# Gate and up products of a SwiGLU block by Strassen's scheme, with float32r operand sums

## The chip, the cores and the metric

The kernel runs on one core of one Trainium2 chip. The metric is device time in microseconds (us) of one execution, as the median of several runs. The profile is of one execution. Its engines are PE (TensorE, matmuls; PEld is its weight load), DVE (VectorE), ACT (ScalarE), POOL (GpSimd) and SP (SyncE, which here only starts DMAs). Each engine works through its own list of instructions in order; between engines there are semaphores.

## The reference

x is 2048 x 512. It is normalised row by row, and two branches of the result are added to x:

```
xn = layernorm(x)
q, k, v = xn @ wqkv                       # 32 heads of 16
pq, pk  = phi(q), phi(k)                  # phi(t) = (t > 0 ? t + 1 : exp(t)) + 1e-6
o = pq (pk^T v) / (pq . sum(pk))          # per head: linear attention
out = x + o @ wo + (silu(xn @ w_gate) * (xn @ w_up)) @ w_down     # hidden width 1792
```

Inputs and output are bf16.

## The kernel before

The 2048 rows are 16 tiles of 128 (t), or 4 chunks of 512 (C = t // 4). The hidden width is 14 pieces of 128 (fc). Everything is written out by hand: a small recorder (`K.add`) takes operations in the order of the text, with the keys that each reads and writes, gives every engine its operations in that order, and derives the semaphore waits. So the order of the text is the order of each engine's list, and an operation that waits holds up all that stands behind it on its engine.

The first stage (0 to about 46 us) is a hand-made list of two-character steps: layernorm of each tile (`bn1`, `bn2`, `rs`, `lna_dve`, `lna_pool`), transposition of the normalised tile into xnT by DMA, projections to q and k (`proj`, line 423), phi (`phi_exp` on ACT, `phi_min` on POOL, `phi_sum` on DVE, line 462), and the accumulation of G = xn^T pk in PSUM banks 0 to 3 (`gacc`, line 472). The projections go round banks 4 to 7. At the end of the list the first gate/up pairs (`pair`) stand between the last G accumulations.

The second stage loops over 56 pairs j = (chunk C, piece fc). A pair is 4 matmuls for gate and 4 for up (`gu`, line 526; stationary a 128x128 piece of the weights, moving 512 columns of xnT), a silu on ACT (line 534) and a product on DVE (`hop`, line 539) that writes a 128x512 piece of hT. The pairs use banks 4 and 5, or 6 and 7, in turn. hT holds two chunks. Between the pairs stand the matmuls of kv (line 584), its mask, M = kv @ wo (line 650), the sum of pk over all rows (z: `z_add` on POOL and DVE, line 495), the denominators (`pz_mul` on POOL, line 617; `divide` and `scale_turn` on DVE, lines 624 to 639), and, from the second chunk on, the output tiles of the chunk before: `ogroup` takes 4 matmuls with M (line 656) and 14 with w_down (line 660) for a tile, `oout` adds x and stores (line 666). z is summed in two halves; of the three tiles whose pk is kept unscaled (0, 1 and 2), `z_add` scales 0 and 1.

Weights and x come by DMAs that SP starts, in the order of the list (`BIG`): w_gate and w_up in halves, the v part of wqkv, wo, and w_down.

Of the kernel before, what the change touches and what calls it, by code (L numbers as in the profile page):

```python
# [6 lines left out]
dt = mybir.dt  # L7
# [22 lines left out]
O_SLOT = {5: 0, 8: 1, 11: 2, 13: 3}  # L30
PZ_AT = {13 + 11 * t // 4: t for t in range(16)}
DIV_AT = {j + 1: t for j, t in PZ_AT.items()}


class _Program:
# [3 lines left out]
    def __init__(self):  # L39
        self.ops = []  # L40
        self.last_w = {}
        self.readers = {}

    def add(self, eng, fns, r=(), w=(), dma=False):
# [4 lines left out]
        for k in r:  # L49
            if k in self.last_w:  # L50
                deps.add(self.last_w[k])
        for k in w:
            if k in self.last_w:
                deps.add(self.last_w[k])
            deps |= self.readers.get(k, set())
        keep = []
        for d in deps:
            o = self.ops[d]
            if o["eng"] == eng and not o["dma"]:
                raw = any(self.last_w.get(k) == d for k in r)  # L60
                if eng == "pe" or not (raw or dma):
                    continue
            keep.append(d)
            o["inc"] = True
# [3 lines left out]
        for k in w:  # L68
            self.last_w[k] = i
            self.readers[k] = set()  # L70
        return i
# [40 lines left out]
def bass_parallel_sum__linear_attn_block__swiglu_ffn__prompt_kernel(nc, A_x, A_wqkv, A_wo, B_x, B_w_gate, B_w_up, B_w_down, out):  # L112
# [5 lines left out]
    with contextlib.ExitStack() as es:  # L118
# [5 lines left out]
        x_sb = sb("x_sb", [P, NT, D], bf)  # L124
        xn = sb("xn", [P, NT, D], bf)
# [7 lines left out]
        xnT = sb("xnT", [P, NDC, S], bf)  # L133
        wqkv = sb("wqkv", [P, NDC, 3 * D], bf)
        wo = sb("wo", [P, NG, D], bf)
        wg = sb("wg", [P, NDC, F], bf)
        wu = sb("wu", [P, NDC, F], bf)
        wd = sb("wd", [P, NFC, D], bf)
        pk = sb("pk", [P, NT, D], bf)
        pq = sb("pq", [P, NT, D], bf)  # L140
        hT = sb("hT", [P, 2, NFC, 512], bf)
        zacc = sb("zacc", [P, 2, D], f32)
        zb = sb("zb", [P, D], bf)
        ef = sb("ef", [P, 6, D], bf)
        GT = sb("GT", [P, NDC, D], bf)
# [3 lines left out]
        pz = sb("pz", [P, 2, D], f32)  # L149
        den = sb("den", [P, 2, NH], f32)  # L150
        rden = sb("rden", [P, 2, NH], f32)
        sil = sb("sil", [P, 2, 512], bf)
        out_sb = sb("out_sb", [P, 2, D], bf)
        ident = sb("ident", [P, P], bf)
        zT = sb("zT", [P, NG, P], bf)
# [9 lines left out]
        xc = hT[:, 1, 0:NC, :]  # L165
        xg = hT[:, 1, NC:2 * NC, :]
        xcT = hT[:, 1, 2 * NC:3 * NC, :].rearrange("p a b -> p (a b)").rearrange("p (c s) -> p c s", c=NDC)
        junk = [hT[:, 1, 3 * NC + t, :] for t in CENTRED]
        zt = pz[:, 0, :]
        shared = {(1, t): [("xc", t, 0), ("xc", t, 1)] for t in CENTRED}  # L170
        shared.update({(1, NC + t): [("xg", t)] for t in CENTRED})
        shared.update({(1, 2 * NC + a): [("xcT", t, h) for t in CENTRED for h in (0, 1)] for a in CENTRED})
        shared.update({(1, 3 * NC + t): [("junk", t)] for t in CENTRED})
        later = {}
        tq = [hT[:, 0, 2 * i:2 * i + 2, :].rearrange("p a b -> p (a b)").bitcast(f32) for i in range(NFC // 2)]
        shared.update({(0, q): [("tq", q // 2)] for q in range(NFC)})
# [22 lines left out]
        def fload(eng, key, dst, src, h):  # L199
            load(eng, (key, h), dst[:, :, h * FH:(h + 1) * FH],  # L200
                 src[:, h * FH:(h + 1) * FH].rearrange("(c p) f -> p c f", p=P))
# [151 lines left out]
        def evac(t, b, eng="act", lo=0, hi=NDC):  # L353
            src = tview(b, hi - lo)
            dst = (xcT if t in CENTRED else xnT)[:, lo:hi, t * P:(t + 1) * P]
# [40 lines left out]

        def xkeys(t):
            return [("xnT", t)]

        def dmat(t):  # L400
            K.add("sp", lambda e: e.dma_start_transpose(out=xnT[:, :, t * P:(t + 1) * P], in_=xn[:, t, :]),
# [11 lines left out]
        def proj(i, t, cs):  # L413
# [4 lines left out]
            src = xcT if t in CENTRED else xnT  # L418
            fns = []
            for c in cs:  # L420
# [3 lines left out]
                    banks[b][:, :], src[:, c, t * P:(t + 1) * P], wqkv[:, c, col:col + D], start=first, stop=last))  # L424
# [6 lines left out]
        def phi_keep(t):  # L431
            b, slot = at[0, t], later[t]
            K.add("act", lambda e: e.activation(tq[slot], banks[b][:, :], ACT.Copy), r=[B(b)], w=[("tq", slot)])

        def phi_exp(i, t):
            b = at[i, t]
            buf, bkey = ef[:, efslot(b), :], ("ef", efslot(b))
            if i == 0 and t in later:
                buf, bkey = pq[:, t, :], ("pq", t)
# [6 lines left out]
        def phi_min(i, t):  # L446
            buf, bkey = ef[:, efslot(at[i, t]), :], ("ef", efslot(at[i, t]))
            if i == 0 and t in later:
                buf, bkey = pq[:, t, :], ("pq", t)
# [5 lines left out]
        def phi_sum(i, t):  # L455
            b = at[i, t]
            dst, dkey = ((pk[:, t, :], ("pk", t)) if i else (pq[:, t, :], ("pq", t)))
            low, lkeys = (flo[:, t:t + 1], [("flo", t)]) if t in CENTRED else (1e-6, [])
            val, mid, keys = banks[b][:, :], ef[:, efslot(b), :], [B(b), ("ef", efslot(b))]
            if i == 0 and t in later:  # L460
                val, mid, keys = tq[later[t]], pq[:, t, :], [("tq", later[t]), ("pq", t)]
            K.add("dve", lambda e: e.scalar_tensor_tensor(  # L462
                out=dst, in0=val, scalar=low, in1=mid, op0=ALU.max, op1=ALU.add),
# [4 lines left out]
        def gacc(t):  # L468
# [4 lines left out]
                banks[c][:, :], src[:, t, c * P:(c + 1) * P], pk[:, t, :],  # L473
# [4 lines left out]
        NZP = 10  # L478

        def z_add(half, i):  # L480
            acc, key = zacc[:, half, :], ("zacc", half)
            t = NZP * half + i
            if half == 0 and i == 1:
                K.add("pool", lambda e: e.tensor_scalar(
                    out=acc, in0=pk[:, 0, :], scalar1=rstd[:, 0:1], scalar2=0.0, op0=ALU.mult, op1=ALU.add),
                    r=[("pk", 0), ("rs", 0)], w=[key])
                K.add("pool", lambda e: e.tensor_scalar(
                    out=zt, in0=pk[:, 1, :], scalar1=rstd[:, 1:2], scalar2=0.0, op0=ALU.mult, op1=ALU.add),
                    r=[("pk", 1), ("rs", 1)], w=[("pz", 0)])
                K.add("pool", lambda e: e.tensor_tensor(out=acc, in0=acc, in1=zt, op=ALU.add),  # L490
                      r=[key, ("pz", 0)], w=[key])
                return
            first, fkey = (pk[:, t - 1, :], ("pk", t - 1)) if i == 1 else (acc, key)
            K.add("dve" if half else "pool",
                  lambda e: e.tensor_tensor(out=acc, in0=first, in1=pk[:, t, :], op=ALU.add),  # L495
                  r=[fkey, ("pk", t)], w=[key])

        def stat(t):
# [14 lines left out]
            "Q": lambda t, cs=range(NDC): proj(0, t, cs), "y": lambda t: phi_exp(0, t), "z": phi_keep, "n": lambda t: phi_min(0, t), "u": lambda t: phi_sum(0, t), "G": gacc, "F": lambda t: keep_busy(t, 256),  # L513
        }

        def gb(j):
            return 4 + 2 * (j % 2)

        def gu(j, extra=(), er=(), ew=()):
            C, fc = j // NFC, j % NFC  # L520
            n = (len(extra) + 7) // 8
            todo = list(extra)
            for b, w_, key in ((gb(j), wg, "wg"), (gb(j) + 1, wu, "wu")):
                fns = []
                for c in range(NDC):
                    fns.append(lambda e, c=c, b=b, w_=w_: e.matmul(  # L526
                        banks[b][:, :], w_[:, c, fc * P:(fc + 1) * P], xnT[:, c, C * 512:(C + 1) * 512],
# [231 lines left out]
```

## Time and profile before

| | |
|---|---|
| three runs | 211.48, 211.82, 211.95 us (median 211.82) |
| span of the profiled execution, first to last instruction | 210.5 us |
| time of the profiled execution beside its span | not given apart from the span |
| PE busy | 207.9 us, 1012 matmuls |
| DVE busy | 124.4 us, 223 instructions |
| ACT busy | 67.2 us, 137 instructions |
| POOL busy | 66.0 us, 92 instructions |
| gate and up matmuls (line 526) | 448 |
| mean granted TensorE clock | 1.000 |

A row of a group reads: line, engine, operation, output <- inputs, shapes, count | busy time in us, mean ns of one | idle time of the engine just before them, and what ended it. A row of the chain or of the timeline begins with its start and its length in us; a timeline row may merge several like instructions (x4). Matmuls are pipelined, so the 379 ns of one overlap with the next.

### The profile page before, as it was taken

Reading aid. Unit: us, or ns where it says so; the run is one execution under the profiler, and the core shown is the slowest. Engines: PE = TensorE matmul, PEld = TensorE weight load, DVE = VectorE, ACT = ScalarE, POOL = GpSimd, SP = SyncE. Lnnn points to the kernel's source line nnn. Section 1 sums busy time; section 2 is a strip of 40 time slices with the busy share of each in tenths; the row PEclk is TensorE's granted clock in tenths of the full one; section 3 lists DMA queues with packets and bytes.
Section 4 is the critical chain, followed back from the end, with each engine's and each line's share of the span. In section 5 each row is a group of like instructions: output and inputs, shape, how many; then the busy total and the mean of one; then the engine's idle time right before and its main releaser. Section 6 shows DMA issues by size and latency. Waiting matters only on the chain.

```text
span 210.5 us, 2725 instructions
## 1 busy us (share of the span) xinstructions
PE 207.9 (99%) x1012; PEld 96.7 (46%) x1012; DVE 124.4 (59%) x223; ACT 67.2 (32%) x137; POOL 66.0 (31%) x92
## 2 busy tenths in 40 slices
PE   8999999999999999999999999999999999999996
PEld 4444444444544444444444444444444444444455
DVE  3999999625995377464554774464457473625122
ACT  5985566644255333021221322130123031220000
POOL 3498876569930152202202121202202220000000
PEclk9999999999999999999999999999999999999999
DMA  5974568699201302010101120111010112011101
GB/s 164 360 231 97 138 101 188 132 344 367 108 0 25 53 0 43 7 50 28 25 25 50 25 30 25 25 50 25 28 31 19 25 50 51 3 50 28 47 28 50
DMA packets 28733, 16.43 MB, mean 78 GB/s; under 512 B 18608, under 2 KB 28592, under 8 KB 28720
## 3 DMA queue, kind: packets, MB, share of 16 engines
q1 hardware_dynamic: 27856, 15.48, 27.8%
q10 hardware_dynamic: 864, 0.79, 1.3%
q8 instruction: 8, 0.13, 0.3%
q14 instruction: 5, 0.04, 0.1%
HBM read 9.96 MB, written 2.10 MB: 57 GB/s over the span
## 4 chain that ended last, share of the span: by engine, by line
PE 99%; DVE 0%; issue 0%
PE pb L526 46%; PE pb L660 23%; PE pb L423 13%; PE pb L656 7%; PE pb L472 7%; PE pb L241 2%; PE pb L384 0%; PE pb L584 0%; PE pb L650 0%; PE pb L376 0%; PE pb L350 0%; DVE out_sb L666 0%
## 5 line engine op out<-in xcount | busy, mean ns | idle before, releaser
L534 ACT ACTIVATE sil<-pb 128x512 bf16<-128x512 f32 x56 | 33.4, 597 | 104.9 <-PE pb L526 103.4
L539 DVE TENSOR_TENSOR hT<-pb,sil 128x512 bf16<-128x512 f32 x56 | 38.2, 683 | 38.0 <-PE pb L526 37.5
L526 PE MATMUL pb<-xnT,wg 128*128 128x512 bf16 x224 | 57.8, 379 | 0.0
L526 PE MATMUL pb<-xnT,wu 128*128 128x512 bf16 x224 | 57.8, 379 | 0.0
L660 PE MATMUL pb<-wd,hT 128*128 128x512 bf16 (+2 forms) x252 | 51.4, 355 | 0.0
L617 POOL TENSOR_TENSOR pz<-pq,zbc 128x512 f32<-128x512 bf16 x16 | 22.3, 1394 | 91.7 <-DVE den L624 79.0
L660 PEld LDWEIGHTS pb<-wd,hT 128*128 128x128 bf16 x252 | 23.5, 98 | 25.0
L526 PEld LDWEIGHTS pb<-xnT,wu 128*128 128x128 bf16 x224 | 21.9, 98 | 25.9
L526 PEld LDWEIGHTS pb<-xnT,wg 128*128 128x128 bf16 x224 | 21.9, 98 | 25.8 <-DVE pq L462 0.2
L666 DVE TENSOR_TENSOR out_sb<-pb,x_sb 128x512 bf16<-128x512 f32 (+2 forms) x18 | 11.4, 633 | 35.8 <-PE pb L660 35.8
L423 PE MATMUL pb<-wqkv,xnT 128*128 128x512 bf16 x104 | 23.9, 379 | 0.0
L444 ACT ACTIVATE ef<-pb 128x512 bf16<-128x512 f32 x26 | 15.1, 593 | 11.6 <-PE pb L423 11.6
L451 POOL TENSOR_SCALAR ef<-ef 128x512 bf16<-128x512 bf16 x26 | 15.9, 618 | 8.5 <-ACT ef L444 8.5
L656 PE MATMUL pb<-M,pk 128*128 128x512 bf16 (+2 forms) x72 | 16.8, 355 | 0.0
L423 PEld LDWEIGHTS pb<-wqkv,xnT 128*128 128x128 bf16 x104 | 10.1, 98 | 12.4 <-issue 0.3
L251 DVE BATCH_NORM_STATS2 stats<-x_sb 128x6 f32<-128x512 bf16 x16 | 10.9, 678 | 3.5 <-DMA x_sb<-in_A_x_dram 3.4
L472 PE MATMUL pb<-pk,xn 128*128 128x512 bf16 x52 | 12.7, 379 | 0.0
L639 DVE TENSOR_TENSOR pq<-pq,rden 128x512 bf16<-128x512 bf16 x16 | 12.6, 786 | 0.0
L624 DVE TENSOR_REDUCE den<-pz 128x32 f32<-128x512 f32 x16 | 10.8, 675 | 0.0
L462 DVE SCALAR_TENSOR_TENSOR pq<-pb,ef 128x512 bf16<-128x512 f32 x13 | 8.7, 679 | 3.0 <-POOL ef L451 3.0
L462 DVE SCALAR_TENSOR_TENSOR pk<-pb,ef 128x512 bf16<-128x512 f32 x13 | 8.9, 683 | 2.7 <-POOL ef L451 2.7
L495 POOL TENSOR_TENSOR zacc<-zacc,pk 128x512 f32<-128x512 f32 x8 | 10.2, 1279 | 0.6
(72 smaller groups left out, 109.5 us busy)
## 6 DMA issues: line engine op xcount, KB each, us to landing
out_dram<-out_sb SPq DMA_DIRECT2D x15, 128.0 KB, 1.7
x_sb<-in_A_x_dram SPq DMA_DIRECT2D x14, 128.0 KB, 4.5
wu<-in_B_w_up_dram SPq DMA_DIRECT2D x2, 896.0 KB, 9.0
wg<-in_B_w_gate_dram SPq DMA_DIRECT2D x2, 896.0 KB, 8.9
wd<-in_B_w_down_dram SPq DMA_DIRECT2D x1, 1792.0 KB, 10.7
wqkv<-in_A_wqkv_dram ACTq DMA_DIRECT2D x4, 128.0 KB, 4.9
wqkv<-in_A_wqkv_dram SPq DMA_DIRECT2D x4, 128.0 KB, 4.7
wqkv<-in_A_wqkv_dram SPq DMA_DIRECT2D x1, 512.0 KB, 4.9
```

Source lines behind the costliest of these rows:

```text
L423: fns.append(lambda e, c=c, first=first, last=last: e.matmul(banks[b][:, :], src[:, c, t * P:(t + 1) * P], wqkv[:, c, col:col + D], start= ...
L444: K.add("act", lambda e: e.activation(buf, banks[b][:, :], ACT.Exp), r=[B(b)], w=[bkey])
L451: K.add("pool", lambda e: e.tensor_scalar(out=buf, in0=buf, scalar1=top, scalar2=0.0, op0=ALU.min, op1=ALU.max), r=[bkey] + tkeys, w=[bkey])
L462: K.add("dve", lambda e: e.scalar_tensor_tensor(out=dst, in0=val, scalar=low, in1=mid, op0=ALU.max, op1=ALU.add), r=keys + lkeys, w=[dkey])
L472: K.add("pe", [(lambda e, c=c: e.matmul(banks[c][:, :], src[:, t, c * P:(c + 1) * P], pk[:, t, :], start=first, stop=last)) for c in range ...
L526: fns.append(lambda e, c=c, b=b, w_=w_: e.matmul(banks[b][:, :], w_[:, c, fc * P:(fc + 1) * P], xnT[:, c, C * 512:(C + 1) * 512], start=(c ...
L534: K.add("act", lambda e: e.activation(sil[:, j % 2, :], banks[gb(j)][:, :], ACT.Silu), r=[B(gb(j))], w=[("sil", j % 2)])
L539: K.add("dve", lambda e: e.tensor_tensor(out=hT[:, C % 2, fc, :], in0=banks[gb(j) + 1][:, :], in1=sil[:, j % 2, :], op=ALU.mult), r=[B(gb( ...
L617: K.add("pool", lambda e: e.tensor_tensor(out=pz[:, t % 2, :].rearrange("q (g p) -> q g p", g=NG), in0=pq[:, t, :].rearrange("q (g p) -> q ...
L639: K.add("dve", lambda e: e.tensor_tensor(out=heads(pq[:, t, :]), in0=heads(pq[:, t, :]), in1=rden[:, i, :][:, :, None].broadcast_to([P, NH ...
L656: fns = [(lambda e, g=g: e.matmul(banks[bank][:, 0:hi - lo], pk[:, t, g * P:(g + 1) * P], M[:, g, lo:hi], start=(g == 0), stop=False)) for ...
L660: fns = [(lambda e, fc=fc: e.matmul(banks[bank][:, 0:hi - lo], hT[:, C % 2, fc, jj * P:(jj + 1) * P], wd[:, fc, lo:hi], start=False, stop= ...
```

## The change

The four chunks are taken as two chunk pairs p, and the 14 pieces as seven piece pairs i. For each (i, p) the gate block xnT[chunks 2p, 2p+1] x w[pieces 2i, 2i+1], split in halves of the inner dimension too, is a 2 x 2 by 2 x 2 block product, and so is the up block. Each is computed with seven products in place of eight (in Winograd's form of Strassen's scheme). A product is two matmuls of 128x128 by 512 columns. The block i = 0, p = 0 is left as it was: four plain pairs (j = 0, 1, 14, 15).

- `x_form` forms, for each chunk pair, four sums or differences of 128x1024 on DVE and a copy on ACT, all as float32r. `w_form` forms, for each piece pair, four differences of the weights (gate and up together, 128x512) and a copy on POOL, as float32r.
- Products 1 and 2 take the bf16 operands as they are; products 3 to 7 take the float32r ones.
- A block uses three PSUM banks of eight (`group`): bank a gets products 1 and 2; ACT copies bank a with product 1 alone into bank b (`fork`), where products 6, 5 and 3 are added; bank c gets product 7, which ACT copies out (`keep7`); DVE writes b + that copy into c (`add_c`), where product 4 is added; DVE writes b with product 5 plus that copy to SBUF (`add_d`), the fourth quarter. silu runs on ACT for the four gate quarters (`q_sil`); the products with up are three on DVE and one on POOL (`q_hop`).
- The order of the second stage is no longer a loop but a list of steps (`STAGE`), in which products of neighbouring blocks alternate; the blocks go in the order (1,0) (1,1) (2,0) (2,1) (3,0) (3,1) (4,0) (4,1) (5,0) (6,0) (5,1) (6,1) (0,1).
- hT is kept whole (56 KB a partition). To make room, tensors share addresses (`region` tells the recorder which); w_down is loaded after the first chunk pair's sums are used up, and x is loaded a second time, into the place of the second pair's sums, by 16 DMAs on ACT's queue.
- The down projection of all 16 tiles follows the second stage. The denominators of tiles 0 to 3 are made in the stage, the others four tiles ahead of their use.
- In the first stage the sums of chunk pair 0 (`H`) and the combinations of piece pair 1 (`V`) are put in at the end; the first halves of w_gate and w_up are loaded before the v part and wo.
- z is summed tile by tile on POOL or DVE, and tile 2 is now scaled like tiles 0 and 1.

The core of the diff:

```diff
+        def w_form(i, k):
+            ring = RING[i]
+            out = TT[ring][k][:, :, :, :]
+            keys = [(w, fc // 7) for w in W_KEYS for fc in (2 * i, 2 * i + 1)]
+            if k == 0:
+                K.add("pool", lambda e: e.tensor_copy(out, quad_w(i, 1, 1)), r=keys, w=[("T", ring, k)])
+                return
+            a, b, op = {1: (quad_w(i, 0, 1), quad_w(i, 0, 0), []), 2: (quad_w(i, 1, 1), TT[ring][1][:, :, :, :], [("T", ring, 1)]),
+                        3: (quad_w(i, 1, 1), quad_w(i, 0, 1), []), 4: (quad_w(i, 1, 0), TT[ring][2][:, :, :, :], [("T", ring, 2)])}[k]
+            K.add("pool", lambda e: e.tensor_tensor(out=out, in0=a, in1=b, op=ALU.subtract), r=keys + op, w=[("T", ring, k)])
+
+        def x_form(p, k):
+            Ca, Cb = 2 * p, 2 * p + 1
+            out = SS[p][k][:, :, :]
+            A11, A12, A21, A22 = xnT[:, Ca, 0:2, :], xnT[:, Ca, 2:4, :], xnT[:, Cb, 0:2, :], xnT[:, Cb, 2:4, :]
+            ka, kb = chunk_keys(Ca), chunk_keys(Cb)
+            if k == 4:
+                K.add("act", lambda e: e.activation(out, A22, ACT.Copy), r=kb, w=[("S", p, k)])
+                return
+            a, b, op, keys = {0: (A21, A22, ALU.add, kb), 1: (SS[p][0][:, :, :], A11, ALU.subtract, [("S", p, 0)] + ka),
+                              2: (A11, A21, ALU.subtract, ka + kb), 3: (A12, SS[p][1][:, :, :], ALU.subtract, [("S", p, 1)] + ka)}[k]
+            K.add("dve", lambda e: e.tensor_tensor(out=out, in0=a, in1=b, op=op), r=keys, w=[("S", p, k)])
+
+        def group(m, i, p):
+            n = groups.setdefault((m, i, p), len(groups))
+            return n % 2, 2 + n % 3, 5 + n % 3, n // 2 % 2
+
+        def product(k, m, i, p):
+            a, b, c, _ = group(m, i, p)
+            if k in (1, 2):
+                fns = [(lambda e, h=h: e.matmul(
+                    banks[a][:, :], wgu[:, m, 2 * (k - 1) + h, 2 * i * P:(2 * i + 1) * P], xnT[:, 2 * p, 2 * (k - 1) + h, :],
+                    start=(k == 1 and h == 0), stop=(h == 1), skip_group_check=(k == 2))) for h in (0, 1)]
+                K.add("pe", fns, r=chunk_keys(2 * p) + [(W_KEYS[m], 2 * i // 7)], w=[B(a)])
+                return
+            tk, sk, bank = {3: (0, 3, b), 4: (4, 4, c), 5: (1, 0, b), 6: (2, 1, b), 7: (3, 2, c)}[k]
+            fns = [(lambda e, h=h: e.matmul(
+                banks[bank][:, :], TT[RING[i]][tk][:, m, h, :], SS[p][sk][:, h, :],
+                start=(k == 7 and h == 0), stop=(h == 1), skip_group_check=(k != 7))) for h in (0, 1)]
+            K.add("pe", fns, r=[("T", RING[i], tk), ("S", p, sk)], w=[B(bank)])
+
+        def fork(m, i, p):
+            K.add("act", lambda e: e.activation(banks[b][:, :], banks[a][:, :], ACT.Copy), r=[B(a)], w=[B(b)])
+        def keep7(m, i, p):
+            K.add("act", lambda e: e.activation(mid[:, m, :], banks[c][:, :], ACT.Copy), r=[B(c)], w=[("mid", m)])
+        def add_c(m, i, p):
+            K.add("dve", lambda e: e.tensor_tensor(out=banks[c][:, :], in0=banks[b][:, :], in1=mid[:, m, :], op=ALU.add),
+                  r=[B(b), ("mid", m)], w=[B(c)])
+        def add_d(m, i, p):
+            K.add("dve", lambda e: e.tensor_tensor(out=end[:, m, :], in0=banks[b][:, :], in1=mid[:, m, :], op=ALU.add),
+                  r=[B(b), ("mid", m)], w=[("end", m)])
...
-            G3 Q4 S14 x4 x9 P5 S7 m4 s4 G13 R7 y4 P10 u13 m9 l12 R14 n4 D5 S8 G4 D10 T2 Q9 s9 P2 S6 K5 x5 u4 S15
+            G3 Q4 S14 x4 x9 P5 S7 m4 s4 G13 R7 y4 P10 u13 m9 l12 R14 n4 D5 S8 G4 D10 T0 Q9 s9 P2 S6 K5 x5 u4 S15
...
-            Q11 s11 y15 K12 y11 u6 x12 G7 m12 G6 n11 Q12 y12 G8 s12 D2 T6 n12 n15 G12 u12 U0 G11 G15 u15 u11
-            U1 T4 T5
+            Q11 s11 y15 K12 y11 u6 x12 G7 m12 G6 n11 Q12 y12 G8 s12 D2 n12 n15 V1 V3 G12 H0 u12 U0 H2 G11 G15 u15
+            u11 H4 V2 V4 V0 U14 H1 H3 T4 T5
...
+zp8 Ea0 Ev3 Uu1 S4 S2 Ug1 t02 Ea1 1g10 zv0 zp9 7g10 Us1 S0 Ea2 t32 Zg10 Uh1 Ug15 Ag10 zv1 t12 S1 6g10 Us15 kvm
+Uu15 zp10 cg10 1u10 Uh15 2g10 t22 Au10 7u10 S3 sa10 4g10 6u10 zp11 Zu10 zv2 5g10 sc10 2u10 cu10 t42 1g11 dg10
+7g11 Ag11 ha10 5u10 Zg11 t05 3g10 zv3 4u10 sd10 du10 t35 6g11 sb10 1u11 hc10 2g11 cg11 Au11 hd10 7u11 sa11 zv4
...
+        for t in range(NT):
+            K.add("act", lambda e, t=t: e.dma_start(x2[:, t, :], xin[t * P:(t + 1) * P, :]), w=[("x2", t)], dma=True)
+        NDIV = 4
+        for t in range(NT - 1):
+            if t + NDIV < NT:
+                pz_mul(t + NDIV)
+            if t not in OPENED:
+                o_h(OB[t % 4], t, 0, D, range(NFC), True, False)
+            o_a(OB[t % 4], t, 0, D, False, True)
+            if t + NDIV < NT:
+                divide(t + NDIV)
+                scale_turn(t + NDIV)
+            oout(OB[t % 4], t, 0, D)
```

In the list, a step of the first stage is a letter and a tile (H, V and U are sums, combinations and plain pairs). In `STAGE`, `6u41` is product 6 of the up block (4,1); `A`, `Z`, `c`, `d`, `s`, `h` are fork, keep7, add_c, add_d, silu and hop; `S` and `t` are sums of chunk pair 1 and combinations; `U` a part of a plain pair (`Ug15` carries kv's matmuls); `E` a copy of G; `zp` and `zv` z sums on POOL and DVE.

467 lines of the change are left out of this document (298 added, 169 removed).

## The prediction

> **What bounds the kernel now.** The page was read first, for the span and the shares; then the chain of work that ended last.
>
> ```profile
> span 210.5 us, 2725 instructions
> PE 207.9 (99%) x1012; PEld 96.7 (46%) x1012; DVE 124.4 (59%) x223; ACT 67.2 (32%) x137; POOL 66.0 (31%) x92
> ...
> PE   8999999999999999999999999999999999999996
> ...
> DVE  3999999625995377464554774464457473625122
> ...
> PE 99%; DVE 0%; issue 0%
> ```
>
> TensorE (PE) is busy from end to end, and the chain is PE alone. PE's busy time is no measure of its pace, since matmuls overlap in the pipe; the pace is read from the chain in order of time (start, length, what), and the two gate/up rows are read in the groups kept apart by shape.
>
> ```profile
> 63.56 20.72 PE pb L526 x96
> ```
> ```profile
> L526 PE MATMUL pb<-xnT,wg 128*128 128x512 bf16 x224 | 57.8, 379 | 0.0
> L526 PE MATMUL pb<-xnT,wu 128*128 128x512 bf16 x224 | 57.8, 379 | 0.0
> ...
> L526 PEld LDWEIGHTS pb<-xnT,wu 128*128 128x128 bf16 x224 | 21.9, 98 | 25.9
> ```
>
> 96 matmuls of 512 columns in 20.72 us are 0.2158 us each, and no idle time stands before any of the 448 gate/up matmuls. The weight loads (98 ns) lie beside the matmul before. So a matmul removed is worth 0.2158 us, as long as nothing makes PE wait; and every wait put on PE is paid in full.
>
> The profiled execution's own time is not shown apart from its span of 210.5; the median of the three runs is 211.82, 1.3 above the span. I sum against the span and add 1.3.
>
> **The change, part by part.**
>
> *Matmuls.* Before, gate and up are 56 pairs of (chunk, fc) with 8 matmuls each: 448. After, four pairs stay plain (32 matmuls). The other 52 pairs are 13 blocks of 2 fc by 2 chunks, and each block takes, for gate and for up, 7 products of 2 matmuls: 13 x 2 x 14 = 364. That is 396, or 52 fewer: 52 x 0.2158 = **11.2 us off PE**. The projections, the G accumulation, M and the down projection keep their counts.
>
> *The float32r matmuls.* Products 3 to 7 (260 matmuls) take float32r operands, which no row of before shows. From below, nothing suggests that they go faster than bf16: 0.2158. From above, by the nearest rows: if the 98 ns load is no longer hidden, 0.314 (260 x 0.098 = +25.5 us); if the stream goes by bytes, twice 0.2158 (260 x 0.2158 = +56 us). I take 0.2158: the moving operand has as many columns, and 98 ns leaves room for a load of twice that length in a pitch of 0.2158.
>
> The Trainium skill speaks against that margin: "TensorE: Matmul & The Clock Gate", section "Weight-path perf modes", says that the fast weight load brings nothing for fp32 and about halves a load otherwise. If the 98 ns above are the fast kind, the slow kind would by that page be an estimated 196 ns, still under the pitch but nearly all of it; no run here shows one. "FP8 and Floating Point Precision", section "TensorE Precision Notes", has true FP32 in four passes and a reduced FP32 read that it gives no passes for; four passes would be 260 x 3 x 0.2158 = 168 us more, by that page alone.
>
> *Operand sums on DVE.* Eight sums of chunk halves (x_form, 128x1024 to float32r) go on VectorE (DVE), two copies on ACT, and 35 weight combinations (w_form) on GpSimd (POOL). All that the first blocks need stands between 44 us and about 70 us. What does such a sum cost? Four timeline rows (start, length, engine) show it:
>
> ```profile
> 58.84 1.15 POOL L495 TENSOR_TENSOR zacc<-zacc,pk 128x512 f32<-128x512 f32 x1
> ```
> ```profile
> 58.27 0.68 DVE L590 TENSOR_TENSOR kvT<-pb,maskt 128x512 bf16<-128x512 f32 x1
> 58.87 1.68 DVE L495 TENSOR_TENSOR zacc<-zacc,pk 128x512 f32<-128x512 f32 x1
> 60.46 0.68 DVE L539 TENSOR_TENSOR hT<-pb,sil 128x512 bf16<-128x512 f32 x1
> 61.06 0.68 DVE L495 TENSOR_TENSOR zacc<-zacc,pk 128x512 f32<-128x512 f32 x1
> ```
> ```profile
> 77.12 1.40 POOL L617 TENSOR_TENSOR pz<-pq,zbc 128x512 f32<-128x512 bf16 x1 [1.72 <-DVE den L624]
> ```
> ```profile
> 78.11 0.96 DVE L639 TENSOR_TENSOR pq<-pq,rden 128x512 bf16<-128x512 bf16 x1
> ```
>
> With POOL silent (61.06), a DVE add of two SBUF operands takes 0.68 us. The same add begun at 58.87, while POOL's add ran from 58.84 to 59.99, ended at 60.55: 0.56 after POOL's end. The multiply at 78.11 ended at 79.07, 0.55 after POOL's end at 78.52. So a DVE instruction with two SBUF operands waits out the POOL instruction that is running, then streams for 0.55. A DVE instruction that reads PSUM costs 0.68 and follows its neighbour at 0.60 (58.27 to 58.87, 60.46 to 61.06). A sum twice as long streams 0.53 longer: 0.68 + 0.53 = 1.21 us alone, and on average about half of POOL's 1.15 (0.5) more when POOL is never silent.
>
> POOL is never silent there: in the changed kernel, weight combinations and z sums follow one another from the place where before's POOL starts its z sums.
>
> ```profile
> 46.43 0.69 POOL L484 TENSOR_SCALAR zacc<-pk,rstd 128x512 f32<-128x512 bf16 x1
> ```
>
> Up to the point below there are about ten two-input instructions at 1.15 plus a gap of 0.08 (estimated), and three copies priced as this 0.69: 14.4 us, stretched by every DVE sum that POOL in turn waits out.
>
> *Where PE meets this.* The order of the changed kernel's DVE instructions puts the sums among the instructions that free PE's banks. These rows show where before stands there:
>
> ```profile
> 43.31 0.69 DVE L462 SCALAR_TENSOR_TENSOR pk<-pb,ef 128x512 bf16<-128x512 f32 x1 [1.90 <-POOL ef L451]
> 45.90 0.69 DVE L462 SCALAR_TENSOR_TENSOR pq<-pb,ef 128x512 bf16<-128x512 f32 x1 [1.90 <-POOL ef L451]
> 48.10 0.69 DVE L539 TENSOR_TENSOR hT<-pb,sil 128x512 bf16<-128x512 f32 x1 [1.51 <-PE pb L526]
> 48.71 1.28 DVE L462 SCALAR_TENSOR_TENSOR pq<-pb,ef 128x512 bf16<-128x512 f32 x2
> ```
> ```profile
> 47.83 1.89 PE L472 MATMUL pb<-pk,xn 128*128 128x512 bf16 x8
> 49.56 0.81 PE L526 MATMUL pb<-xnT,wg 128*128 128x512 bf16 x3
> ```
>
> The first sum costs nothing: DVE idles from 44.0 to 45.90 in before. The second stands ahead of the two phi sums of 48.71, and the next gate matmul (49.56) needs their banks: PE's first wait, 1.2 to 1.7 us. I follow the queue to the first PE instruction behind all of it, product 5 of the up half of the first block, which needs that half's add_c. DVE has, from 48.71:
> - seven sums at 1.21: 8.5;
> - nine instructions that read PSUM (two phi sums, the hops of the three later plain pairs, a GT copy, the kvT mask, two add_c) at 0.60: 5.4;
> - three z sums at about 0.6: 1.8.
>
> That is 15.7. Waits for POOL, 0.5 at each of the ten with SBUF operands alone: 5.1. One idle stretch, while the hop of pair 14 waits for matmuls that themselves started late: about 1.3 (1.7 us of matmuls, less two phi sums, plus hand-overs). Together 22.1, so add_c ends at 70.8. PE has 48 matmuls and the 16 short ones of kv in front of that product: 48 x 0.2158 + 16 x 0.055 = 11.2 us (0.055 is a quarter of 0.2158, for 128 columns), so from 49.56 it would be there at 60.8. **PE loses 10.0 us**, in waits of 1 to 3.5 us. Bounds: 4.9 without any POOL wait; 13 if each sum waits a whole POOL instruction (5 more) and queue time covers 2 of it.
>
> What is queued behind PE's wait is all of PE; what is queued behind a DVE sum is the hop or the GT copy on which PE waits next, so none of it is hidden.
>
> *Between 70 and 150 us*, a block of 28 matmuls is 6.04 us of PE. Beside it:
>
> ```profile
> L539 DVE TENSOR_TENSOR hT<-pb,sil 128x512 bf16<-128x512 f32 x56 | 38.2, 683 | 38.0 <-PE pb L526 37.5
> L534 ACT ACTIVATE sil<-pb 128x512 bf16<-128x512 f32 x56 | 33.4, 597 | 104.9 <-PE pb L526 103.4 <-PE pb L584 1.6
> L617 POOL TENSOR_TENSOR pz<-pq,zbc 128x512 f32<-128x512 bf16 x16 | 22.3, 1394 | 91.7 <-DVE den L624 79.0 <-DMA zbc<-zrow 12.6
> ```
>
> DVE: 2 add_c, 2 add_d and 3 hops at 0.60 are 4.2. ACT: 2 forks, 2 keeps and 4 silus at 0.60 are 4.8. POOL, per two blocks (12.1 us of PE): 4 combinations, a copy, 2 hops of the fourth quarter and a z sum, at 1.23 and 0.72: 9.3. An instruction that writes PSUM from DVE or ACT is not in before; I take the rows' prices, bounded by 0 and +0.2. No engine is over PE; I allow 0.5 us for hand-overs.
>
> *The rest.* The down projection moves behind gate/up with the same matmuls, 18 to a tile: 3.88 us.
>
> ```profile
> L639 DVE TENSOR_TENSOR pq<-pq,rden 128x512 bf16<-128x512 bf16 x16 | 12.6, 786 | 0.0
> ...
> L624 DVE TENSOR_REDUCE den<-pz 128x32 f32<-128x512 f32 x16 | 10.8, 675 | 0.0
> ...
> L635 DVE RECIPROCAL rden<-den 128x32 f32<-128x32 f32 x16 | 5.6, 353 | 0.6
> ```
> ```profile
> wd<-in_B_w_down_dram SPq DMA_DIRECT2D x1, 1792.0 KB, 10.7
> ```
>
> Beside a tile, DVE has these (0.79, 0.68, 0.35), a short add and an out of 0.69: about 2.7; POOL has one pz of 1.39. The down weights now load into space that the first sums hold, so they are asked for late: 31 products (31 x 2 x 0.2158 = 13.4 us) before use, against 10.7 to land. x is loaded a second time on ACT's queue after its last silu; its first use may be late, but three tiles (11 us) pass before that bank is needed again. On SP's queue the first gate load moves ahead of the v weights, and both are needed no earlier than in before. The scaled z of tile 2 is one DVE instruction, counted above. All nothing, hidden by PE; without that cover the down weights cost what they are late, at most a few us.
>
> Sum: 210.5 - 11.2 + 10.0 + 0.5 = 209.8 of span, **211.1 us** with the 1.3. The saving is real and nearly all of it is given back before 71 us.
>
> **The rivals.**
>
> *POOL is seldom in the way* (faster). If the collisions don't meet these sums, DVE's list is 17.0 and PE loses 4.9: 204.7 + 1.3 = 206.0. For it: POOL waits too, and gaps may line up. Against: both rows above show the full wait.
>
> *Hand-overs in every block* (slower). An add_c must be done before the product that adds to its bank; PE has 3 or 4 products (1.3 to 1.7 us) between. With one DVE instruction ahead (0.60 + 0.69, and about 0.2 of hand-over) it is just in time; with two it is 0.5 late. At 0.2 us for 26 halves, 5.2 us: 216.3. It decides once DVE's PSUM writers take over about 0.8 us, or POOL's combinations cost pz's 1.39 instead of 1.15. Against it: 4.2 of 6.04.
>
> *The float32r matmul doesn't keep bf16's pitch* (slower): with the load exposed, 211.1 + 25.5 = 236.6; with a doubled stream, 267. The change then saves no PE time. For it: twice the bytes for both operands. Against it: the stretch of 98 ns in 0.2158.
>
> **How the numbers follow.** Forecast 0.47 (its own range 209 to 213.2), collisions seldom 0.14 (204.5 to 209), hand-overs 0.22 (213 to 219.5), slow float32r 0.17 (above 220). The predicted time is 211.1. The range 205.0 to 220.0 leaves out the last case and little else. A measurement of this kernel tells about 0.2% from no change, so faster is below 211.40 and slower above 212.24. Within the forecast's own range about 0.28 of the 0.47 lies below, 0.10 between and 0.09 above. Faster: 0.28 + 0.14 = 0.42. Same: 0.10. Slower: 0.09 + 0.22 + 0.17 = 0.48.
>
> **What would show it.** The pitch of product matmuls in a stretch without waits: 0.216 bears the forecast out, 0.31 or 0.43 the last rival. The chain of waits: PE's idle time should lie between 49 and 72 us, about 10 us, ended by DVE; the length of the x_form rows: 1.2 when POOL is silent, up to 2.2 beside it. After 72 us, PE idle under 1 us; several us there, ended by DVE's add_c, is the second rival. I am wrong if PE is idle before 49 us, or if the down projection waits for its weights or for x's second load.

## The result, and the profile after

| | before | after |
|---|---|---|
| median of four runs each, us | 211.72 (211.48 to 211.95) | 216.95 (216.53 to 217.79) |
| profiled execution: time / span, us | 211.48 / 210.5 | 216.53 / 215.2 |
| ratio, 95% interval | | 1.0247 (1.0219 to 1.0275) |

The change makes the kernel 2.5% slower. The forecast was 211.1, 0.7 us below the 211.82 from which it reckoned. The profiled executions differ by 4.7 us of span, and it is these that the following accounts for.

The page of the changed kernel, in 40 slices of 5.4 us:

```profile
span 215.2 us, 2788 instructions
PE 203.7 (95%) x943; PEld 112.7 (52%) x960; DVE 165.2 (77%) x269; ACT 94.4 (44%) x192; POOL 122.3 (57%) x140
...
PE   8999999996648999999999999999999999999996
...
DVE  3899998647899987677777779999379999975112
...
PEclk9999999999996999999999999999999999999999
...
PE 88%; DVE 8%; DMA 2%; issue 1%; ACT 0%
```

960 matmuls are left of 1012 (the 960 weight loads; 17 matmul records are missing), so the 52 are saved. PE now has one hole, in the slices from 48 to 70 us (6, 6, 4, 8), where DVE is busy for seven to nine tenths; and the granted clock falls in the last of them. The chain was PE alone, and is now 8% DVE. The chain of work through that hole, in order of time (start, length, what):

```profile
49.04 0.69 DVE hT L665
49.73 2.15 DVE S L700
51.88 0.61 DVE pq L586
...
52.54 1.91 PE pb L649 x8
...
54.48 0.69 DVE hT L665
55.17 1.62 DVE S L700
...
56.81 2.07 DVE S L700
58.88 0.60 DVE GT L786
59.48 1.50 DVE S L700
60.97 1.30 DVE zacc L611
62.28 2.10 DVE S L700
...
64.90 1.03 DVE zacc L613
65.93 2.10 DVE S L700
68.03 0.61 DVE kvT L795
...
68.69 2.28 PE pb L717 x8
```

From 49 to 68.7 us the end is set by DVE's queue, but for one pair of PE (52.54). Six of the operand sums (S, line 700) stand in the chain with 1.5 to 2.15 us each, and z sums (zacc) between them. This is the wait list of PE (us in total, times, longest):

```profile
PE pb L649 <- DVE hT L665: 3.8, 2, 3.0
PE pb L649 <- DVE pq L586: 1.8, 1, 1.8
PE pb L649 <- ACT pb L724: 1.6, 1, 1.6
...
PE pb L557 <- DMA xnT<-xn: 0.5, 1, 0.5
PE pb L717 <- DVE kvT L795: 0.3, 1, 0.3
```

After the hole nothing stops PE. The chain there is a repetition of half blocks, 10 float32r matmuls (L717) and 4 bf16 ones (L711):

```profile
101.77 2.31 PE pb L717 x10
104.09 0.88 PE pb L711 x4
104.97 2.31 PE pb L717 x10
...
114.55 2.31 PE pb L717 x10
```
```profile
L717 PEld LDWEIGHTS pb<-S,T 128*128 128x128 f32 x260 | 48.5, 188 | 14.6 <-DVE kvT L795 1.0
```

Four half blocks take 114.55 - 101.77 = 12.78 us, so one takes 3.195, where 14 x 0.2158 would be 3.02. PE doesn't wait for any of it: the whole change pays 26 x 0.175 = **4.5 us** in matmuls that are themselves slower. The weight load has gone from 98 ns to 188.

And the first gate matmul comes later than in before (first row before, second row after):

```profile
46.10 1.03 PE L526 MATMUL pb<-xnT,wg 128*128 128x512 bf16 x4
```
```profile
47.12 1.24 PE L649 MATMUL pb<-xnT,wgu 128*128 128x512 bf16 x5
```

That is 1.0 us. On its way there PE waits once for a transposed tile:

```profile
29.84 2.76 PE L557 MATMUL pb<-wqkv,xnT 128*128 128x512 bf16 x12 [0.53 <-DMA xnT<-xn]
```

The account of the 4.7: -11.2 (52 matmuls) + 4.5 (float32r) + 1.0 (first stage) leaves 10.4 for the hole. This is a remainder; read directly, PE takes 21.57 us from the first gate matmul (47.12) to the first product behind kvT (68.69). The 50 matmuls of 512 columns and 16 of 128 between them would take 50 x 0.2158 + 16 x 0.055 = 11.7, so 9.9 are lost there, and 0.5 of the 10.4 isn't placed. Of the 9.9, 7.5 are the waits of the list, 1.5 the halved clock, and some 0.8 that a wait's idle time, which begins at the end of a matmul's 0.38 us, leaves out of the pitch (5 x 0.16). The eight matmuls at the halved clock, 0.42 us apart, are these:

```profile
65.03 1.89 PE L649 MATMUL pb<-xnT,wgu 128*128 128x512 bf16 x4 [3.02 <-DVE hT L665]
66.71 1.70 PE L711 MATMUL pb<-xnT,wgu 128*128 128x512 bf16 x4
```

### The profile page after: what moved, and what is told of

Its sections match the earlier page's. It is cut to its first block, busy times and chain, and to the rows that moved or that the text cites. A ratio compares the mean times of both kernels' runs of the same rounds, so it can differ in the third digit from the quotient of the medians.

```text
span 215.2 us, 2788 instructions
## 1 busy us (share of the span) xinstructions
PE 203.7 (95%) x943; PEld 112.7 (52%) x960; DVE 165.2 (77%) x269; ACT 94.4 (44%) x192; POOL 122.3 (57%) x140
## 4 chain that ended last, share of the span: by engine, by line
PE 88%; DVE 8%; DMA 2%; issue 1%; ACT 0%
PE pb L717 28%; PE pb L861 22%; PE pb L557 12%; PE pb L711 10%; PE pb L867 6%; DVE S L700 5%; PE pb L596 5%; DMA xnT<-xn 2%; PE pb L649 2%; PE pb L372 2%; DVE hT L665 1%; DVE zacc L611 1%; DVE zacc L613 0%; PE pb L515 0%; PE pb L507 0%
## 5 line engine op out<-in xcount | busy, mean ns | idle before, releaser
L717 PE MATMUL pb<-S,T 128*128 128x512 f32 x260 | 70.7, 415 | 0.3 <-DVE kvT L795 0.3
L717 PEld LDWEIGHTS pb<-S,T 128*128 128x128 f32 x260 | 48.5, 188 | 14.6 <-DVE kvT L795 1.0
L753 DVE TENSOR_TENSOR hT<-pb,sil 128x512 bf16<-128x512 f32 x39 | 26.6, 682 | 10.9 <-PE pb L717 10.4
L753 POOL TENSOR_TENSOR hT<-end,sil 128x512 bf16<-128x512 f32 x13 | 15.1, 1161 | 24.8 <-DVE end L737 22.6
L711 PE MATMUL pb<-xnT,wgu 128*128 128x512 bf16 x98 | 26.6, 389 | 0.3
L724 ACT ACTIVATE pb<-pb 128x512 f32<-128x512 f32 x26 | 15.2, 584 | 25.8 <-PE pb L711 25.8
L737 DVE TENSOR_TENSOR end<-pb,mid 128x512 f32<-128x512 f32 x26 | 17.7, 681 | 5.3 <-PE pb L717 5.3
L688 POOL TENSOR_TENSOR T<-wgu 128x512 fp32r<-128x512 bf16 x14 | 18.5, 1328 | 4.6 <-PE pb L717 4.3
L732 DVE TENSOR_TENSOR pb<-pb,mid 128x512 f32<-128x512 f32 x26 | 18.0, 692 | 2.0 <-PE pb L717 2.0
L688 POOL TENSOR_TENSOR T<-wgu,T 128x512 fp32r<-128x512 bf16 x14 | 17.8, 1276 | 0.1
L728 ACT ACTIVATE mid<-pb 128x512 f32<-128x512 f32 x26 | 15.6, 600 | 1.0 <-DVE end L737 0.5
L711 PEld LDWEIGHTS pb<-xnT,wgu 128*128 128x128 bf16 x104 | 8.6, 100 | 13.6 <-issue 7.1
```

What stands on the lines that cost most here:

```text
L688: K.add("pool", lambda e: e.tensor_tensor(out=out, in0=a, in1=b, op=ALU.subtract), r=keys + op, w=[("T", ring, k)])
L711: fns = [(lambda e, h=h: e.matmul(banks[a][:, :], wgu[:, m, 2 * (k - 1) + h, 2 * i * P:(2 * i + 1) * P], xnT[:, 2 * p, 2 * (k - 1) + h, :] ...
L717: fns = [(lambda e, h=h: e.matmul(banks[bank][:, :], TT[RING[i]][tk][:, m, h, :], SS[p][sk][:, h, :], start=(k == 7 and h == 0), stop=(h = ...
L732: K.add("dve", lambda e: e.tensor_tensor(out=banks[c][:, :], in0=banks[b][:, :], in1=mid[:, m, :], op=ALU.add), r=[B(b), ("mid", m)], w=[B ...
L737: K.add("dve", lambda e: e.tensor_tensor(out=end[:, m, :], in0=banks[b][:, :], in1=mid[:, m, :], op=ALU.add), r=[B(b), ("mid", m)], w=[("e ...
L753: K.add("pool" if q == 3 else "dve", lambda e: e.tensor_tensor(out=hT[:, C, fc, :], in0=src, in1=sils[r][:, q, :], op=ALU.mult), r=[key, ( ...
```

## The experiments

The theories at this point: (1) float32r operands make the products' matmuls longer; (2) the gate load, moved ahead of the v part, delays x's transposes; (3) DVE's queue of sums, z sums and waits for POOL makes PE wait between 49 and 72 us; (4) the halved clock behind PE's longest wait costs 1.7 us of its own. The main rival is the prediction's: hand-overs between DVE, ACT and PE in every block.

**The order of the loads** (e1_loads).

```diff
-... D10 T0 ... R11 T2 ... m11 T3 ...
+... D10 T2 ... R11 T3 ... m11 T0 ...
```

> The changed kernel with the order of the weight loads on SP's queue as it was before: the v part of the projection weights goes out first, the output weights second, the first half of the gate weights third. All else is the changed kernel. If the 896 KB gate load, which the change sends out ahead of the v part, holds up x's DMA transposes, the first gate matmul starts at 46.1 us as in before and not at 47.1, and the time falls by 1.0, to 215.9. If the 1.0 us in front of 47 us comes from the new places of the tiles in memory or from the scaled z of tile 2, the first gate matmul still starts at 47.1 and the time stays at 217.0.

Measured: 216.96 (215.34 to 217.12), ratio to before 1.0217 (1.0191 to 1.0243). The first gate matmul starts at 46.47 and PE's wait for a transpose is gone (one of 0.5 us for projection weights stands in its place), but the time is that of the changed kernel. The timeline of PE shows what took the gain:

```profile
65.44 1.91 PE L711 MATMUL pb<-xnT,wgu 128*128 128x512 bf16 x4
68.06 3.78 PE L717 MATMUL pb<-S,T 128*128 128x512 f32 x8 [0.70 <-DVE kvT L795]
```

Eight product matmuls at 68.06 take 3.78 us, where the changed kernel's eight took 2.28 (68.69 in its chain). The clock stayed halved there for twice as long, 6.8 us (65.1 to 71.9). This experiment alone settles nothing about the loads; the pair below does.

**bf16 in place of float32r** (e3_bf16).

```diff
-        f32r = dt.float32r
+        f32r = bf
```

> The changed kernel with every float32r tile made bf16: the operand sums are rounded to bf16 and products 3 to 7 run in bf16. Instructions, their order and their waits stay. If the operand type sets the pitch of the products, the half block of 14 matmuls goes from 3.19 us to 3.02, the product's weight load from 188 ns to 98, and 26 halves give 4.4 us back: 212.5, with the waits between 49 and 72 us as they were; if the sums also stream faster in 16 bits, up to 4 us less on top: 208.5. If the pitch of 0.231 comes from DVE and ACT writing the banks beside PE (hand-overs in every block), the half block stays at 3.19 us and the time at 217.

Measured: 208.88 (208.43 to 209.38), ratio 0.9853 (0.9832 to 0.9874): 8.1 us less than the changed kernel, and 1.5% faster than before. The chain and two of DVE's sums, the first without and the second beside POOL:

```profile
96.47 2.16 PE pb L717 x10
98.63 0.86 PE pb L711 x4
```
```profile
44.80 0.68 DVE L700 TENSOR_TENSOR S<-xnT 128x1024 bf16<-128x1024 bf16 x1
...
49.52 1.70 DVE L700 TENSOR_TENSOR S<-xnT 128x1024 bf16<-128x1024 bf16 x1
```

The half block is 3.02 us: all 4.5 us of theory 1 are the operands' type. The other 3.6 fit the sums: with 16-bit output one takes 0.68 us alone, where the float32r one takes 1.21, and seven in the queue are 7 x 0.53 = 3.7. DVE ends the up half's add_c 21.4 us after the first gate matmul, where it took 25.1, and PE's waits fall from 7.5 to 4.6. The Trainium skill has, in "VectorE: DVE Perf Modes", section "The perf-mode tier table", a `tensor_tensor` at twice the single rate on bf16 in SBUF, and at the single rate on fp32. 0.68 against 1.21 agrees, if 0.15 of each is a fixed part; here the result alone changed its type.

**What a float32r matmul costs alone** (e6_pitch, e12_switch): spare matmuls behind the last one of PE's queue, where no other engine works on PE's banks.

```diff
+        for f32 in (True, False):
+            for n in (512, 256):
+                def spare(e, f32=f32, n=n):
+                    ...
+                    return e.matmul(banks[6][:, 0:n], w, x, start=True, stop=True)
+                K.add("pe", [spare] * 24, ...)
```

> The changed kernel with 96 spare matmuls put at the end of PE's queue, where DVE, ACT and POOL have nothing left that writes PE's banks: 24 float32r of 512 columns, 24 float32r of 256, 24 bf16 of 512, 24 bf16 of 256. The time is meaningless; the pitches are read. If the float32r weight load (188 ns) sets the pitch, 512 columns take 0.23 us here too, and 256 columns are no faster than 0.19 to 0.21, while bf16 takes 0.216 and 0.108 to 0.12. If the float32r stream itself is 7% slower and the load is hidden, 512 columns take 0.231 and 256 take 0.116. If the 0.231 of the products comes from DVE and ACT writing banks beside PE, float32r takes 0.216 for 512 columns here.

Measured, in the timeline of PE, float32r of 512 and 256 columns (the second row begins with one of 512 and is labelled by it), then bf16 of 512:

```profile
215.25 5.39 PE L948 MATMUL pb<-S 128*128 128x512 f32 x23
```
```profile
220.25 3.14 PE L948 MATMUL pb<-S 128*128 128x512 f32 x24
```
```profile
223.35 5.14 PE L948 MATMUL pb<-hT 128*128 128x512 bf16 x23
```

Less the last one's own length (0.389 and 0.379), 22 steps of 512 columns are 5.00 us in float32r and 4.76 in bf16: 0.227 and 0.216. For 256 columns it is (3.14 - 0.227 - 0.283) / 22 = 0.120; bf16 gave 0.109. So both expected mechanisms fall: a float32r matmul is about **11 ns longer at both widths**. A stream 7% slower would have given 0.116; a load of 188 ns that sets the pitch would not allow 0.120. The prediction cited the Trainium skill's "TensorE: Matmul & The Clock Gate", section "Weight-path perf modes", for an estimated 196 ns of slow load: the load is indeed of that length (188), and it doesn't show in the pitch.

11 ns for ten of fourteen matmuls make 0.11 of the 0.175. For the rest, groups of 10 float32r and 4 bf16:

> The changed kernel with eight groups of 10 float32r and 4 bf16 matmuls of 512 columns, on fixed operands, at the end of PE's queue: the mixture of a half block without DVE, ACT and POOL beside it. The time is meaningless; the period of a group is read. 10 x 0.2267 + 4 x 0.2163 = 3.13 us if only the float32r matmuls themselves are longer; then the half block's 3.19 holds 0.06 that comes from work on other engines. 3.19 if the change of type costs 0.06 for each turn there and back.

Measured, in the chain:

```profile
216.63 12.71 PE pb L948 x55
...
229.41 10.39 PE pb L948 x45
```

With one missing record (a step of 0.07 marked as issue), 56 matmuls or four groups take 229.41 - 216.63 = 12.78 us: 3.195 a group, the period of the changed kernel's half blocks to the digit. So 0.06 goes to each turn from one type to the other and back, and nothing to DVE or ACT writing PE's banks. That the pitch comes from other engines' writes to the banks is excluded by this.

**The z sums out of the transition** (e5_zlate): the tokens zv0 to zv4 and zp8 to zp12 moved behind later products.

```diff
-zp8 Ea0 Ev3 Uu1 S4 S2 Ug1 t02 Ea1 1g10 zv0 zp9 7g10 ... zv1 ... zp10 ... zp11 Zu10 zv2 ...
+Ea0 Ev3 Uu1 S4 S2 Ug1 t02 Ea1 1g10 7g10 ... hd11 zp8 zv0 ... hb11 zp9 zv1 ... hd20 zp10 zv2 ...
```

> The changed kernel with the z sums taken out of the transition: the five on DVE (tiles 0 to 4) and POOL's five for tiles 8 to 12 go into the blocks after about 75 us, as many instructions as in the changed kernel. If DVE's queue and its waits for POOL make PE wait between 49 and 72 us, the list up to the up half's first add_c loses four z sums at 0.6 and up to 0.5 each of waiting for POOL, 2.4 to 4.4 us, and PE's waits there fall from 8.6 to 4.2 to 6.2 us; one or two us may come back where the z sums stand now. The time: 213 to 216. If the waits are those of the plain pairs' own hand-overs (matmul, silu, hop), nothing changes there and the time is 217 or more.

Measured: 213.33 (213.14 to 213.62), ratio 1.0066 (1.0051 to 1.0082): 3.6 us less than the changed kernel. PE's waits between 49 and 72 us fall from 7.5 to 6.1 (ACT's fork 2.1, hops 2.0, phi sums 1.8, kvT 0.2), and the clock stays at 1.00. The profiled spans differ by 3.3 us (215.2 and 211.9), of which 1.4 are these waits and 1.5 the halved clock that is gone. (The 7.5 is the sum of the list above; the 8.6 of the expectation is not.) DVE ends the up half's add_c 21.6 us after the first gate matmul, where the changed kernel took 25.1, as theory 3 has it. POOL didn't become silent: its weight combinations moved up into the place of the z sums, and the sums of line 700 still take up to 2.25 us.

**POOL silent as well** (e8_quiet): from there, POOL's combinations for the third block moved behind POOL's hop of the first.

```diff
-... t02 ... t32 ... t12 ... t22 ... t42 ... hd10 7u11 ...
+... hd10 t02 t32 t12 t22 t42 7u11 ...
```

> The kernel with the late z sums, and POOL's five weight combinations for the third block moved behind POOL's hop of the first block's up half, so that POOL stands still from about 56 us until that hop. If DVE's sums are long because they wait out POOL's instructions, every sum begun while POOL stands still takes 1.21 us instead of 1.6 to 2.2, and PE's idle time between 49 and 72 us falls from 6.1 us by a further 2 to 4. If the sums are long for another reason, they stay at 1.6 to 2.2 and the idle time at 6. The time itself may gain nothing, since the moved combinations are late for the third block: 5 combinations at 1.15 us, up to 5 us given back after 72 us: 210 to 216.

Measured: 212.58 (212.14 to 212.85), ratio 1.0022 (1.0005 to 1.0038). POOL idles from 54.7 to 67.3 us (first row), and DVE's timeline there has:

```profile
67.26 1.16 POOL L753 TENSOR_TENSOR hT<-end,sil 128x512 bf16<-128x512 f32 x1 [12.60 <-DVE end L737]
...
54.61 1.21 DVE L700 TENSOR_TENSOR S<-S,xnT 128x1024 fp32r<-128x1024 f32 x1
55.85 1.22 DVE L700 TENSOR_TENSOR S<-xnT,S 128x1024 fp32r<-128x1024 bf16 x1
...
64.53 0.69 DVE L732 TENSOR_TENSOR pb<-pb,mid 128x512 f32<-128x512 f32 x1
```

Every sum in that stretch takes about 1.2 us, and the up half's add_c ends at 65.2, or 18.6 us after the first gate matmul. PE's waits there fall to 3.2. That DVE's sums are long because POOL works beside them is shown by this; that they wait out the running instruction, the changed kernel's rows show. The sum that its chain has from 62.28 to 64.38 ended 1.09 us after this instruction of POOL, which ended at 63.29:

```profile
61.96 1.33 POOL L688 TENSOR_TENSOR T<-wgu,T 128x512 fp32r<-128x512 bf16 x1
```

Against the late z sums that is 2.9 us less of waiting; 1.6 of it is given back after 85 us, in waits for the late combinations (0.8) and for DVE (0.8). The medians differ by 0.75 only, and the rest is not placed.

**The clock** (e7_clock): 12 spare matmuls of 512 columns on constants (F3, into bank 3) in PE's longest wait.

```diff
-... kvm
-Uu15 zp10 ...
+... kvm
+F3 Uu15 zp10 ...
```

> The changed kernel with 12 spare bf16 matmuls of 512 columns (constants, written to a bank that is free there) in PE's queue in front of the up product of pair 15, the one that waits 3.4 us. They take 2.6 us of that idle time; nothing else is changed. If the clock is halved by the idle time, the eight matmuls behind it run at 0.216 to 0.231 instead of 0.427 us and the time falls by 1.7, to 215.3. If those eight are slow for another reason (their operands just written, bank hand-overs), they stay at 0.427 and the time at 217.0; if PE were not idle there, the spare matmuls would cost up to 2.6: 219.6.

Measured: 216.25 (216.17 to 216.48), ratio 1.0202 (1.0184 to 1.0220). The clock theory is right about the mechanism and wrong about the price. PE's timeline:

```profile
64.71 1.04 PE L649 MATMUL pb<-xnT,wgu 128*128 128x512 bf16 x4 [0.37 <-DVE hT L665]
65.58 1.03 PE L711 MATMUL pb<-xnT,wgu 128*128 128x512 bf16 x4
68.37 1.80 PE L717 MATMUL pb<-S,T 128*128 128x512 f32 x6 [1.76 <-DVE kvT L795]
```

The eight matmuls run at full speed, in 1.90 us instead of 3.38, and then PE stands 1.76 us for DVE's kvT instead of 0.28. The first product behind kvT starts 21.6 us after the first gate matmul in both kernels (68.37 - 46.78, 68.69 - 47.12). So it does in e6_pitch and e12_switch, which are the changed kernel up to there: the eight matmuls happened to run at full speed, PE stood 1.76 us for kvT, and the product came after 21.6 us again. The half clock lay beside DVE's queue and cost nothing in the profiled execution of the changed kernel. The median of its four runs does hold some of it: the two with a mean clock of 0.992 took 216.53 and 216.67 us, the two with 0.984 (as in e1_loads) 217.24 and 217.79.

**Another order, alone and with bf16** (e10_order, e9_best). The two phi sums go ahead of the second operand sum (`U0 G11 G15 u15 u11 H2 H4` for `U0 H2 G11 G15 u15 u11 H4`), the loads are as in before, and z sums, combinations and the sums for chunk pair 1 stand where DVE and POOL have time; the list begins so:

```diff
-zp8 Ea0 Ev3 Uu1 S4 S2 Ug1 t02 Ea1 1g10 zv0 zp9 7g10 Us1 S0 Ea2 t32 Zg10 Uh1 Ug15 Ag10 zv1 t12 S1 6g10 Us15 kvm
-Uu15 zp10 cg10 1u10 Uh15 2g10 t22 Au10 7u10 S3 sa10 4g10 6u10 zp11 Zu10 zv2 5g10 sc10 2u10 cu10 t42 1g11 dg10
+zp8 Ea0 Ev3 Uu1 zp11 Ug1 zv0 t02 Ea1 1g10 zp9 7g10 Us1 S0 Ea2 Zg10 Uh1 Ug15 Ag10 t12 S1 6g10 Us15 kvm Uu15 zp10
+cg10 1u10 Uh15 2g10 t22 Au10 7u10 sa10 4g10 6u10 Zu10 S2 t05 5g10 sc10 2u10 cu10 S4 1g11 dg10 7g11 Ag11 ha10
```

> The changed kernel with its arithmetic as it is, float32r products included, and another order: the loads as in the kernel before, the two phi sums ahead of the second operand sum, and the z sums, the weight combinations and the sums for chunk pair 1 spread over the blocks in which DVE and POOL have time. If the transition's 10 us come from DVE's queue there, PE's idle time between 49 and 72 us falls to about 4 us and the time to 210 to 211.5; the pitch stays at 0.231 and keeps 4.4 us above what the matmul count gives. If the waits are of another origin, the time stays near 217 less 0.6 for the loads: 216.3.

> The same other order with the operand sums and products 3 to 7 in bf16 as well. If the two causes are separate, this is the order's gain and the type's together: pitch 0.216, sums 0.68 us alone, PE's idle time between 49 and 72 us under 2.5 us, and 203 to 206 us, below both kernels. If the shorter sums had already taken away the waits that the order takes away, it stays at the 208.9 of bf16 alone, less 0.6.

Measured: 209.14 (208.73 to 209.31) in float32r, ratio 0.9869 (0.9853 to 0.9886), with PE's waits between 49 and 72 us at 2.4, both better than expected; and with bf16 203.71 (203.37 to 203.88), ratio **0.9608** (0.9594 to 0.9623), faster than both kernels. The waits of PE that are left in the bf16 version, in that stretch:

```profile
PE pb L649 <- DVE hT L665: 1.8, 2, 1.0
...
PE pb L649 <- ACT GT L784: 0.5, 1, 0.5
```

The order, the loads' 1.0 included, is worth 7.8 us against the changed kernel, without a change in its arithmetic; the type then another 5.4, of which 4.5 are the pitch. The pitch is thus a cause by itself. The sums' length and their place overlap by 2.7: bf16 alone gave 8.1.

**The loads once more, without a halved clock** (e11_noloads against e10_again): the same order in float32r, with the gate load ahead of the v part again.

> The kernel with the other order in float32r, with the weight loads put back into the changed kernel's order (the first gate load ahead of the v part), and nothing else. Run beside the same kernel with the loads of before, without a halved clock in either. If the gate load holds up x's transposes, the first gate matmul starts 0.6 to 1.0 us later and the time rises by as much, to 209.8 to 210.1. If that start only varies by chance from one execution to the next, the two times agree within 0.2 us.

> The other order in float32r once more, with the loads of before, as the partner of the kernel with the loads moved: 209.1, as measured.

Measured, side by side: 210.08 (209.54 to 210.29) and 209.03 (209.03 to 209.13), ratios to before 0.9906 (0.9888 to 0.9924) and 0.9863 (0.9845 to 0.9881). The first gate matmul of each:

```profile
46.88 0.81 PE L649 MATMUL pb<-xnT,wgu 128*128 128x512 bf16 x3
```
```profile
46.10 1.67 PE L649 MATMUL pb<-xnT,wgu 128*128 128x512 bf16 x7
```

And this wait stands in the list of the first and not in that of the second:

```profile
PE pb L557 <- DMA xnT<-xn: 0.6, 2, 0.4
```

The moved load costs 0.8 us of the start, and the medians differ by 1.05. All traces agree: with the load moved (eight of them) the first gate matmul starts between 46.55 and 47.47, and PE waits for a transpose in each; with the loads of before (five) it starts between 45.76 and 46.47, and PE never does. Theory 2 holds.

## Why the prediction was wrong

Its sum was 210.5 - 11.2 + 10.0 + 0.5 = 209.8 of span, against 215.2. Point by point:

- **"Matmuls"**, 52 fewer at 0.2158: right. The half blocks of the bf16 version run at 3.02, exactly 14 x 0.2158.
- **"The float32r matmuls ... I take 0.2158": the step that failed**, by 4.5 us of a miss of 5.4. Both of its upper bounds thought of a cost per byte or per load (25.5 and 56 us), and the lower bound was taken because the load of twice 98 ns would still fit. It does fit: 188 ns. What was not in view is a small fixed cost, 11 ns a matmul and 0.06 a turn between the types. Times 26 half blocks, it is 40% of the whole saving. The rival "doesn't keep bf16's pitch" was priced at 26 us or more, so there was nothing between 0 and 25.5.
- **"PE loses 10.0"**: right in place and in size, and DVE's queue is the cause. add_c of the up half was put at 70.8 and ended at 72.2 (71.2 but for the late start); the hole is 10.4. Two details were otherwise: PE's waits are 7.5 of it, since the halved clock filled 1.5 of the idle time, and PE's last wait was for kvT (68.64), after which add_c came just in time. The price of a sum (1.21 alone, longer beside POOL) is as forecast, and so are the waits in the main (0.3 to 3.0 us, where 1 to 3.5 were said), and e8_quiet and e5_zlate show the two terms of the list by taking them out one after the other.
- **"The rest ... both are needed no earlier than in before"**, at nothing: wrong by 0.8 to 1.0. The sentence asked when the gate weights are needed, and not what their 896 KB hold up on their way: x's transposes, on which PE's projections wait at 29 us. "I am wrong if PE is idle before 49 us" was the right alarm.
- **"0.5 for hand-overs"**: too much by 0.5; nothing of it is seen after 72 us.
- The half clock was not foreseen. It cost nothing in the profiled execution, since DVE's queue ended later anyway; with a second halved stretch behind it, in e1_loads, it cost about 1.5 us (3.78 for 2.28).

Of the rivals, "POOL is seldom in the way" is refuted by the chain and by e8_quiet, "hand-overs in every block" by PE's empty wait list after 72 us (that its 216.3 lies near the measured time is chance), and "float32r doesn't keep bf16's pitch" was right in kind and far off in price.

The miss in span is 215.2 - 209.8 = 5.4: 4.5 for float32r, 1.0 for the load and 0.4 for the hole, less the 0.5 for hand-overs. (The hole's 10.4 is the remainder, so that this adds up is no proof; the 9.9 read directly bears it out.) The chances had slower at 0.48, but by the edge of the forecast's range and two rivals that both turned out otherwise. The lesson is in the margin: a saving of 11.2 with 10.0 given back has a remainder of 1.2, and the two edits priced at nothing cost 4.5 and 1.0. The sign hung on the steps that were set at nothing.

## What to carry to other kernels

A scheme that saves matmuls with another operand type is to be priced by that type's pitch in a mixture like the kernel's, measured on spare matmuls: 0.175 us in 3.02 is easily overlooked, and it is paid in every block. New work for an engine that isn't the bound is dear where it comes all at once: PE waited 7.5 us with all the sums in front of the first block and 2.4 with only what the next product needs ahead of it. When a load is moved up in a queue, ask what it delays, not when it is needed.

## What the runs showed of the hardware

- A float32r matmul (128x128 by 512) takes 0.227 us against 0.216 for bf16, and 0.120 against 0.109 with 256 columns; its weight load takes 188 ns against 98. Ten of them with four bf16 ones take 3.195 us, which is 0.06 more than the parts.
- Behind a wait of 3.0 us, PE's clock was halved for 3.4 us in the changed kernel (64.7 to 68.1, matmuls 0.42 apart), and for 6.8 in e1_loads, where a second gap of 0.7 us fell into the halved stretch. The Trainium skill describes this in "TensorE: Matmul & The Clock Gate", Part 1: a free-running window of about 3.4 us that is counted as idle halves the clock. The lengths here, one window and two, agree; e7_clock, with the gap filled, kept the full clock. A whole window without work isn't needed: in e3_bf16 a halved stretch followed a wait of 2.0 us, while e5_zlate, whose longest wait is 2.1, had none. The same wait of 3.0 us was followed at once by the half clock in the changed kernel, and in e6_pitch and e12_switch only at 70.5 and 69.7 us, behind the next wait.
- A DVE sum of two bf16 operands of 128x1024 takes 0.68 us with a bf16 result and 1.21 with a float32r one; beside POOL 1.0 to 1.7, and 1.5 to 2.25.
